# Orders written as tables, weights in four pieces and other gates for the loads in a gated linear attention and MLP kernel

## The chip, the cores and the metric

The kernel runs on one core of one Trainium2 chip. The metric is the time of one execution on the device in microseconds; of several runs the median is given. Profiles show one execution, in microseconds from the start of its span.

## What is computed

Four batches of eight heads, 768 tokens, head size 48. A state of 48 x 48 per head decays by alpha and takes in an outer product at every token; the output of all heads, 3072 tokens of 384 numbers, goes through two layers with a squared relu between them.

```python
for t in range(S):
    state = alpha[:, :, t, :, None] * state + np.einsum('bhd,bhe->bhde', k[:, :, t], v[:, :, t])
    y[:, :, t] = np.einsum('bhd,bhde->bhe', q[:, :, t], state)
...
x = np.ascontiguousarray(attn_out.transpose(0, 2, 1, 3)).reshape(B * S, H * D)
h = x @ w_in            # 384 x 2048
r = np.maximum(h, 0.0)
out = (r * r) @ w_out   # 2048 x 384
```

All inputs and the output are float32 in device memory; the matmuls run in bf16.

## The kernel before

**Units.** The work is cut into 12 units of 256 tokens: three stretches of the sequence, four batches each, in the order stretch 0 of all batches, stretch 1, stretch 2. Names of operations end in the unit's number.

**One unit.** Four loads (`lda`, `ldk`, `ldq`, `ldv`: alpha, k, q, v, 384 KB each). The front takes the logarithm of alpha on ScalarE (`ln`; for most units on the product `pr` of two neighbouring tokens), sums it along the tokens by matmuls (`m1`, `m1i`, `m1s`), takes exponentials (`ei`, `ea`, `ec`, `es`), and multiplies them into k and q on VectorE (`ekm`, `eqm`, with `bk` and `aq` for the neighbouring token). The products are transposed: on TensorE with a copy out of PSUM for units 0 to 2 (`tr`, `et`), by DMA for the others (`tr0_3`, `tr1_3` and so on). `vc` casts v to bf16. Then come the scores (`p`, masked by `mk` on VectorE), the state (`kv`, `sa`, `sc`, `sd`), the output of the attention (`y`, copied out by `xe`) and its transposition (`xt`, `xv`; by DMA from unit 4 on). Unit 0 does its front in two halves of four heads: `ln0_0`, `ln1_0`, `ei0_0` and so on up to the score parts `p0_0` and `p1_0`.

**The two layers of a unit.** The first is eight blocks `s1_g_u` of six matmuls each, into one of two PSUM banks in turn. Each block is emptied by a relu (`re`, ScalarE or VectorE) and squared in pairs or alone (`sq`, VectorE, ScalarE or POOL). The second is eight blocks `s2_g_j_sg` of four matmuls, four for each half j of the tokens, summed in a single PSUM bank `psO` which `oe` empties; then `out` stores it. The last 128 tokens of unit 11 go by two cuts of the columns (line 1012).

**Who decides the order.** Every operation is entered with `add`, with its engine or engines to choose from, a cost and a due time (`prio`). `schedule` plays the program through with these costs, a picture of the DMA rings among them, and picks for each free engine the ready operation with the lowest due time; a table `SHIFT` moves single due times, `BIAS` holds POOL back, and `AFFINITY` lets TensorE go on with one kind of matmul. What comes out is a fixed list for each engine, emitted in that order: on the chip each engine goes through its list and waits at each entry for what it needs. `fill` then puts filler matmuls on zeros (line 1143) into the gaps of TensorE's list, from the landing of the memset of ZERO up to the planned start of the first s1 block. All operations without a name (memsets, masks) are entered first.

**Loads.** The loads of a unit go through SP's queue, except those of unit 2, which POOL issues. The weights are cast from float32 to bf16 in the DMA and so are issued by POOL as well, in `WS` pieces each: `win0`, `win1`, `wout0`, `wout1`. A load or a weight piece can have a gate: another load whose landing it waits for before it is issued (`AFTER`). Every piece of `win` covers `FT / WS` of the 16 blocks of 128 hidden numbers, so s1 blocks 0 to 3 need `win0` and 4 to 7 `win1`; the s2 blocks with sg 0 and 1 need `wout0`, those with 2 and 3 `wout1`.

```python
AFTER = {(1, "v"): (0, "q"), ("win", 0): (1, "a"), ("win", 1): (1, "a"), 2: (1, 'v'), ("wout", 0): (1, 'v'),
         ("wout", 1): (1, 'v'), 3: ("wout", 0)}
AFTER.update({g: (g - 1, "q") for g in range(4, G)})
```

From unit 5 on, a load also waits for the last reader of the unit before (`BEHIND`).

**The list of the start before the change.** TensorE: nine fillers, `m10_0 m11_0`, four fillers, `tr00_0`, fillers, `tr10_0`, fillers, `tr01_0 p0_0 kv0 tr11_0`, fillers, `p1_0 m11`, fillers, `y0`, fillers, `tr0_1 xt0`, fillers, `tr1_1`, fillers, `p0_1 s1_0_0 s1_0_1 kv1 s1_0_2 s1_0_3 y1 s1_0_4 s1_0_5 xt1 s1_0_6 s1_0_7 m1i2 s1_1_0 ...`. POOL: masks, `vc0 win0 win1 sd0 lda2 ldk2 ldq2 ldv2 wout0 wout1 sd1 pr3 sd2 vc4 pr5 vc5 pr6 vc7 vc10`. SP: the eight loads of units 0 and 1, then `lda3 ldk3 ldq3 ldv3 lda4 ldk4 ldq4 ldv4 out0_1 tr0_3 tr1_3 lda5 ...`.

Of the kernel before, what the change touches and what calls it, by code (L numbers as in the profile page):

```python
# [33 lines left out]
class Program:  # L34
# [12 lines left out]
    AFFINITY = 2500

    SHIFT = {
        "aq2": -248, "aq3": -1491, "bk2": 5224, "bk3": -2010, "bk5": 1601, "bk6": -3855, "ea0_0": 13157,  # L50
        "ea1": -1949, "ea1_0": 12558, "ea2": 2000, "ea3": -1980, "ea4": -1414, "ea5": -2487, "ea6": 81,
        "ec0_0": 20747, "ec1": -746, "ec1_0": 11544, "ec2": 2000, "ec3": -2160, "ec4": -1533, "ec5": 2471,
        "ei0_0": 10906, "ei1": -1289, "ei1_0": 11939, "ei2": 2000, "ei3": 8259, "ei4": -2378, "ei5": 98, "ei6": -386,
        "ekm0_0": 11970, "ekm1": -1066, "ekm1_0": 10619, "ekm2": 5424, "ekm3": -1183, "ekm4": 175, "ekm5": 937,
        "ekm6": 1068, "eqm0_0": 12087, "eqm0_3": -1862, "eqm0_4": 3228, "eqm0_5": 3013, "eqm0_6": -440, "eqm1": 2398,
        "eqm1_0": 12786, "eqm1_3": 1310, "eqm1_4": 270, "eqm1_5": -275, "eqm1_6": -211, "eqm2": 2240, "es2": 2000,
        "es3": -2890, "es5": -2113, "es6": -1558, "et00_0": -6783, "et01_0": 2965, "et0_1": 18, "et0_2": 4740,
        "et10_0": 1180, "et11_0": 849, "et1_1": -8121, "et1_2": 9290, "kv0": 1952, "kv1": -5798, "kv2": -10315,
        "lb4": -1797, "lb5": 195, "lb6": 67, "lm4": -1578, "lm5": -1529, "lm6": -1532, "ln0_0": 10550, "ln1": -409,
        "ln1_0": 17073, "ln2": 2000, "ln3": -2160, "ln4": 564, "ln5": 4370, "ln6": -283, "m10_0": 4838, "m11": -338,  # L60
        "m11_0": 9538, "m1i2": 2121, "m1i3": -533, "m1i5": 400, "m1i6": -1147, "m1s2": 2468, "m1s3": 3167,
        "mk0_0": -1001, "mk0_1": 9322, "mk0_2": 5670, "mk0_3": -10630, "mk0_4": 4794, "mk0_5": -4832, "mk1_0": -830,
        "mk1_1": 1380, "mk1_2": 4510, "mk1_3": -10630, "mk1_4": 7108, "mk1_5": -124, "oe0_0": -3484, "oe0_1": -14385,
        "oe1_0": -724, "oe1_1": 2594, "oe2_0": -260, "oe2_1": -627, "oe3_0": 11805, "oe3_1": 30, "oe4_0": -7260,
        "oe4_1": -7260, "oe5_0": 5260, "oe5_1": 5260, "out0_1": -8010, "out1_1": 6560, "out2_1": 2593, "out3_1": 30,
        "out4_1": -7260, "out5_1": 5260, "p0_0": -830, "p0_1": -2249, "p0_2": 4532, "p0_3": -11271, "p0_4": 2163,
        "p0_5": -6910, "p1_0": -830, "pr2": 376, "pr3": 563, "pr4": -2031, "pr5": 4470, "pr6": -3765, "pr7": -5581,
        "re0_0": -253, "re0_1": -2327, "re0_2": -1810, "re0_3": -2805, "re0_4": 7066, "re0_5": -3141, "re0_6": 1463,
        "re0_7": -2710, "re1_0": -2540, "re1_1": -1766, "re1_2": -2620, "re1_3": -2792, "re1_4": 4740, "re1_5": 99,
        "re1_6": -833, "re1_7": 2948, "re2_0": -151, "re2_1": -240, "re2_2": 24, "re2_3": -68, "re2_4": -519,  # L70
        "re2_5": -240, "re2_6": 5363, "re2_7": 3246, "re3_0": -3327, "re3_1": -1860, "re3_2": -1860, "re3_3": -2293,
        "re3_4": -1860, "re3_5": -5935, "re3_6": -6334, "re3_7": -1379, "re4_0": -5850, "re4_1": -2100,
        "re4_2": -6410, "re4_3": -2118, "re4_4": -5850, "re4_5": -5850, "re4_6": -5850, "re4_7": -5850,
        "re5_0": 2020, "re5_1": 2020, "re5_2": 2020, "re5_3": 2020, "re5_4": 2020, "re5_5": 2020, "re5_6": 2020,
        "re5_7": 2020, "s1_0_0": -2767, "s1_0_1": -1766, "s1_0_2": -1810, "s1_0_3": -1898, "s1_0_4": 202,
        "s1_0_5": -2691, "s1_0_6": -5306, "s1_0_7": 405, "s1_1_0": -2620, "s1_1_1": -5074, "s1_1_2": -364,
        "s1_1_3": 596, "s1_1_5": -6169, "s1_1_6": -383, "s1_1_7": -1034, "s1_2_0": -739, "s1_2_1": -687,
        "s1_2_2": -5198, "s1_2_3": -900, "s1_2_4": -1700, "s1_2_5": -240, "s1_2_6": -45, "s1_2_7": -688,
        "s1_3_0": -1860, "s1_3_1": -2146, "s1_3_2": -1582, "s1_3_3": -1860, "s1_3_4": -3211, "s1_3_5": -435,
        "s1_3_6": -1113, "s1_3_7": -1860, "s1_4_0": -10307, "s1_4_1": -5990, "s1_4_2": -5519, "s1_4_3": -6913,  # L80
# [316 lines left out]
def bass_gla_recurrent__then__act_relu_squared_kernel(  # L397
# [777 lines left out]
```

## Time and profile before

| what | value |
|---|---|
| median of 3 runs | 174.92 us (174.46 to 176.85) |
| the profiled execution: own time / span | 176.21 us / 174.5 us |
| busy: TensorE, its weight loads | 169.1 us, 130.5 us |
| busy: VectorE, ScalarE, POOL | 121.3 us, 117.6 us, 18.8 us |
| HBM read, written | 25.17 MB, 4.72 MB |
| queue 1 (loads, stores, transposes), share of 16 DMA engines | 71.4% in 73184 packets |
| queue 0 (issued by POOL's software, the weights among them) | 12.1% in 1536 packets |

Busy time counts a matmul from its start to its end, and matmuls overlap, so the distance from one start to the next says more than the length. A transfer has an issue (an instruction on SP or POOL) and a landing; the view of a tile gives the time between the two. A wait is put down to what ended it last.

### The profile page before, as it was taken

Reading aid. Unit: us, or ns where it says so; the run is one execution under the profiler, and the core shown is the slowest. Engines: PE = TensorE matmul, PEld = TensorE weight load, DVE = VectorE, ACT = ScalarE, POOL = GpSimd, SP = SyncE. Lnnn points to the kernel's source line nnn. Section 1 sums busy time; section 2 is a strip of 40 time slices with the busy share of each in tenths; the row PEclk is TensorE's granted clock in tenths of the full one; section 3 lists DMA queues with packets and bytes.
Section 4 is the critical chain, followed back from the end, with each engine's and each line's share of the span. In section 5 each row is a group of like instructions: output and inputs, shape, how many; then the busy total and the mean of one; then the engine's idle time right before and its main releaser. Section 6 shows DMA issues by size and latency. Waiting matters only on the chain.

```text
span 174.5 us, 5094 instructions
## 1 busy us (share of the span) xinstructions
PE 169.1 (97%) x2237; PEld 130.5 (75%) x2237; DVE 121.3 (70%) x197; ACT 117.6 (67%) x211; POOL 18.8 (11%) x28
## 2 busy tenths in 40 slices
PE   7989999999999999999999999999999999999994
PEld 2556898856886697777788886778788697688773
DVE  5497799797967869866778966868849726322230
ACT  3848698868869569768768757378668564566440
POOL 3159010022102120000100000000200000000000
DMA  5999999979998999798998897999899690040022
GB/s 139 324 297 190 274 303 216 230 208 280 274 229 125 274 235 188 200 222 151 278 212 211 228 196 180 275 201 251 201 214 208 115 196 4 0 135 4 10 80 90
DMA packets 74743, 33.36 MB, mean 191 GB/s; under 512 B 71649, under 2 KB 71905, under 8 KB 74721
## 3 DMA queue, kind: packets, MB, share of 16 engines
q1 hardware_dynamic: 73184, 28.32, 71.4%
q0 software_dynamic: 1536, 4.72, 12.1%
q8 instruction: 17, 0.28, 0.7%
q14 instruction: 6, 0.04, 0.1%
HBM read 25.17 MB, written 4.72 MB: 171 GB/s over the span
## 4 chain that ended last, share of the span: by engine, by line
PE 56%; DMA 26%; ACT 6%; DVE 4%; SPq 3%; POOL 2%; issue 1%
PE psO L1089 22%; PE psWH L1042 22%; DMA raw<-in_v_dram 9%; DMA wout<-in_moe_w_out_dram 8%; DMA raw<-in_alpha_dram 5%; DMA raw<-in_q_dram 5%; SPq L568 3%; PE psO L1143 2%; POOL raw L568 2%; ACT rr L1050 2%; PE psX L843 2%; PE psX L1012 2%; ACT vbf L742 1%; PE psZ L811 1%; PE psX L832 1%; PE psX L940 1%
## 5 line engine op out<-in xcount | busy, mean ns | idle before, releaser
L1042 PE MATMUL psWH<-xt,win 128*128 128x256 bf16 x576 | 73.9, 275 | 0.5 <-ACT rr L1050 0.2
L1042 PEld LDWEIGHTS psWH<-xt,win 128*128 128x128 bf16 x576 | 65.0, 145 | 6.2 <-DVE rr L1052 1.6
L1089 PE MATMUL psO<-wout,gt 128*128 128x384 bf16 x368 | 68.9, 326 | 0.0
L1050 ACT ACTIVATE rr<-psWH 128x512 bf16<-128x512 f32 x83 | 48.9, 596 | 21.5 <-PE psWH L1042 20.0
L1089 PEld LDWEIGHTS psO<-wout,gt 128*128 128x128 bf16 x368 | 34.8, 98 | 18.3 <-DVE gt L1060 0.2
L1060 DVE TENSOR_TENSOR gt<-rr 128x1024 bf16<-128x1024 bf16 (+1 forms) x47 | 28.4, 608 | 25.1 <-ACT rr L1050 24.5
L951 DVE TENSOR_TENSOR pm<-psX,caus 128x1024 bf16<-128x1024 f32 x12 | 14.6, 1220 | 2.4 <-PE psZ L940 2.1
L951 DVE TENSOR_TENSOR pm<-psZ,caus 128x1024 bf16<-128x1024 f32 x12 | 14.6, 1216 | 1.5 <-PE psZ L940 1.4
L1097 ACT ACTIVATE osb<-psO 128x384 f32<-128x384 f32 x19 | 9.3, 489 | 6.8 <-PE psO L1089 6.3
L971 ACT ACTIVATE xbf<-psX 128x768 bf16<-128x768 f32 x12 | 9.7, 806 | 5.0 <-PE psX L832 4.1
L746 DVE TENSOR_TENSOR qks<-raw,eq 128x384 bf16<-128x384 f32 x18 | 10.3, 605 | 3.0 <-DMA raw<-in_q_dram 3.0
L1143 PE MATMUL psO<-zero 128*128 128x512 bf16 (+1 forms) x37 | 10.5, 417 | 1.3 <-DVE zero L489 1.3
L741 POOL CAST vbf<-raw 128x768 bf16<-128x768 f32 x4 | 3.7, 930 | 71.5 <-DMA raw<-in_v_dram 71.5
L1064 ACT ACTIVATE gt<-rr 128x512 bf16<-128x512 bf16 (+1 forms) x13 | 10.8, 828 | 0.4
L751 DVE TENSOR_TENSOR qks<-raw,ek 128x768 bf16<-128x768 f32 x11 | 10.7, 969 | 0.4 <-ACT ek L663 0.3
L1052 DVE TENSOR_SCALAR rr<-psWH 128x512 bf16<-128x512 f32 x13 | 8.9, 687 | 2.0 <-PE psWH L1042 1.6
L742 ACT ACTIVATE vbf<-raw 128x768 bf16<-128x768 f32 x7 | 5.9, 845 | 3.5 <-DMA raw<-in_v_dram 3.5
L717 ACT ACTIVATE la<-raw 128x384 f32<-128x384 f32 x8 | 4.2, 523 | 5.3 <-DMA raw<-in_alpha_dram 5.2
L1143 PEld LDWEIGHTS psO<-zero 128*128 128x128 bf16 x37 | 3.5, 108 | 4.6 <-issue 1.9
L906 DVE TENSOR_TENSOR smd<-psZ,sbd 128x384 bf16<-128x384 f32 x8 | 4.4, 554 | 3.4 <-PE psX L832 3.4
L675 DVE TENSOR_TENSOR prd<-raw 128x384 f32<-128x384 f32 x7 | 4.0, 569 | 2.9 <-DMA raw<-in_alpha_dram 2.9
L678 ACT ACTIVATE lab<-prd 128x384 bf16<-128x384 f32 x10 | 5.2, 520 | 1.1 <-POOL prd L677 0.6
(115 smaller groups left out, 165.9 us busy)
## 6 DMA issues: line engine op xcount, KB each, us to landing
raw<-in_alpha_dram SPq DMA_DIRECT2D x11, 384.0 KB, 4.2
raw<-in_k_dram SPq DMA_DIRECT2D x11, 384.0 KB, 5.1
raw<-in_q_dram SPq DMA_DIRECT2D x11, 384.0 KB, 4.2
raw<-in_v_dram SPq DMA_DIRECT2D x11, 384.0 KB, 4.8
out_dram<-osb SPq DMA_DIRECT2D x11, 384.0 KB, 4.3
win<-in_moe_w_in_dram POOLq DMA_DIRECT2D x2, 768.0 KB, 9.9
wout<-in_moe_w_out_dram POOLq DMA_DIRECT2D x2, 768.0 KB, 15.2
raw<-in_alpha_dram POOLq DMA_DIRECT2D x1, 384.0 KB, 9.7
```

What stands on the lines that cost most here:

```text
L746: add("dve", lambda e, j=j, dst=dst: e.tensor_tensor(dst, RAW[r][:, 2, :, j, :].rearrange("p (n x) d -> p n x d", x=2), EQ[la][:, j].rearr ...
L751: add("dve", lambda e, a=a, E=E: e.tensor_tensor(QKS[qs][:, a, :, :, 0:D], RAW[r][:, 1 + a].rearrange("p h j d -> p j h d"), E[la][:].rear ...
L951: add("dve", lambda e, hf=hf, psT=psT: e.tensor_tensor(PM[pm][:, hf].rearrange("p r n j t -> p (r n) (j t)"), psT[:, :, :].rearrange("p r ...
L971: add("act", lambda e: e.activation(XBF[x2][:], psX[:, :, 0:HD], AF.Copy), act_ns(2 * HD), p0 + 6100, reads=[("ps", "X", 0), ("ps", "X", 1 ...
L1042: ins = pe.matmul(psH[hb][:, i * T:(i + 1) * T], WIN[:, kk, hidden(fj)], mov, start=(kk == 0), stop=(kk == KT - 1))
L1050: add("act", lambda e, hb=hb, rr=rr: e.activation(rr, psH[hb], AF.Relu), act_ns(512), pu + 600, reads=[("ps", "H", hb)], writes=[("rr", rb ...
L1052: alts={"dve": (lambda e, hb=hb, rr=rr: e.tensor_scalar(rr, psH[hb], 0.0, None, ALU.max), dve_ns(512))})
L1060: add("dve", lambda e, dst=dst, sq=sq: e.tensor_tensor(dst, sq, sq, ALU.mult), 148 + k * 267, pu + 1200, reads=[("rr", rb, h) for h in ran ...
L1064: "act": (lambda e, dst=dst, sq=sq: e.activation(dst, sq, AF.Square), act_ns(k * 512))})
L1089: ins = pe.matmul(psS, GT[gt][:, fj, j, :], WOUT[:, fj, :], start=(fj * parts % FT == 0), stop=((fj + 1) * parts % FT == 0))
L1097: add("act", lambda e, j=j, psS=psS: e.activation(OSB[ob][:, j], psS, AF.Copy), act_ns(DM), ps_ + 700, reads=[keyS], writes=[("osb", ob, j ...
L1143: pr.fill(lambda n: lambda pe: pe.matmul(psO[:, 0:n], ZERO[:, 0:128], ZERO[:, 0:n], skip_group_check=True), ((512, 216, 420), (256, 109, 2 ...
```

## The change

The schedule no longer chooses: `ORDERS` names for every engine all its operations in order, and with that which engine does what. `SHIFT`, `BIAS` and `AFFINITY` go. Fillers are put in as before. Operations without a name get `c` and their number (c1 and c3 are the memsets of LAF, c8 to c13 those of the masks, c14 and c15 two of POOL's masks, c19 the memset of ZERO, c20 to c22 POOL's other masks, c23 a copy on ScalarE). Further:

- both weights come in four pieces instead of two (`WS`), with new gates; s1 blocks 0 and 1 now need `win0`, 2 and 3 `win1` and so on, and the s2 blocks with sg 0 to 3 need `wout0` to `wout3`;
- alpha, k and q of unit 0 are loaded in two halves of four heads;
- the gates: `win0` waits for v of unit 0, the other three pieces of `win` for k of unit 1, unit 3 for `wout1` instead of `wout0`, and unit 4 for `wout3` besides q of unit 3;
- the second layer of units 0 and 1 is done in two parts (`IN_HALVES`): first the blocks with sg 0 and 1, copied out by `oe`; after unit 1's first part, those with sg 2 and 3, which `oa` on VectorE adds to what was copied out. Four additions come in.

```diff
+ORDERS = {
+    "pe": """
+        m10_0 m11_0 tr10_0 tr00_0 tr11_0 kv0 p0_0 tr01_0 m11 p1_0 y0 tr0_1 xt0 tr1_1 s1_0_0 s1_0_1 p0_1 s1_0_2 s1_0_3
+        m1i2 kv1 s1_0_4 s1_0_5 y1 s1_0_6 m1s2 s1_0_7 xt1 tr0_2 s1_1_1 s1_1_0 s1_1_3 s1_1_2 tr1_2 s2_0_0_0 s2_0_0_1
+        p0_2 s1_1_5 m1i3 s2_0_1_0 s2_0_1_1 kv2 s1_1_4 m1s3 s2_1_0_0 s2_1_0_1 s1_1_6 s1_1_7 y2 s2_1_1_0 m1i4 xt2
+        s2_1_1_1 s1_2_0 s1_2_1 s2_0_0_2 s1_2_2 s2_0_0_3 s1_2_3 s1_2_4 s2_0_1_2 s2_0_1_3 m1i5 p0_3 s2_1_0_2 s1_2_6
...
+        s1_11_5 s2_10_1_3 s1_11_6 s1_11_7 s2_11_0_0 s2_11_0_1 s2_11_0_2 s2_11_0_3 s2_11_1_0 s2_11_1_1
+    """.split(),
+    "act": """
+        table ln0_0 ei0_0 ea0_0 ln1_0 c23 ei1_0 ea1_0 et10_0 ec1_0 vc0 ec0_0 ln1 et11_0 et01_0 ei1 ea1 ec1 xe0 re0_0
+        re0_1 sq0_1 ln2 re0_2 re0_3 ei2 ea2 ec2 re0_5 xe1 re0_6 es2 re0_7 sq0_7 re1_1 re1_0 et0_2 et1_2 ln3 re1_2 ei3
...
+    "dve": """
+        c8 c16 c11 c12 c7 c13 c5 c10 c1 c9 c3 ekm0_0 c17 c18 c6 eqm0_0 ekm1_0 eqm1_0 et00_0 c19 sa0 sc0 mk0_0 mk1_0
+        ekm1 eqm1 xv0 c2 et1_1 et0_1 pr2 mk1_1 mk0_1 sa1 sc1 re0_4 bk2 ekm2 xv1 c4 sq0_5 eqm2 sq1_1 sd1 re1_3 pr3
...
+    "pool": """
+        c20 c21 c22 c15 c14 win0 lda2 win1 win2 win3 ldk2 wout1 vc1 sd0 ldq2 wout0 sq0_3 ldv2 aq2 wout3 vc2 sq1_3 bk3
+        wout2 pr5 sq2_3 sq1_7 bk5 sd3 sq3_5 sq3_7 vc6 sd5 pr7 sq4_5 sq4_7 sq5_3 bk8 pr9 sq6_1 sq6_3 vc9 pr10 sq7_1
+        vc10 pr11 sq7_7 sd6 sq8_1 bk11 sq8_3 sd7 sq9_3 sq10_7 sq11_3 sq11_5 sq11_7
+    """.split(),
+    "sp": """
+        lda0_0 ldq0_1 lda0_1 ldk0_1 ldk0_0 ldq0_0 ldv0 lda1 ldv1 ldk1 ldq1 lda3 ldq3 ldk3 ldv3 lda4 ldq4 ldk4 lda5
+        tr0_3 tr1_3 ldv4 ldk5 tr0_4 tr1_4 ldq5 ldv5 out1_1 out0_1 lda6 tr0_5 ldk6 tr1_5 ldq6 xt4 ldv6 lda7 ldk7 tr0_6
...
-    BIAS = {"pool": 300}
-    DMA_LAST = {"sp": 800, "act": 800, "pool": 1900}
+    DMA_LAST = {"sp": 800, "act": 800, "pool": 1500}
...
-    AFFINITY = 2500
-
-    SHIFT = {
...
-        op = Op(choices, prio + self.SHIFT.get(name, 0), name)
+        op = Op(choices, prio, name or f"c{len(self.ops)}")
...
+        place = {n: (e, k) for e, names in ORDERS.items() for k, n in enumerate(names)}
+        for op in self.ops:
+            e = place[op.name][0]
+            op.alts = {e: op.alts[e]}
...
-    WS = 2
+    WS = 4
...
-    IN_HALVES = ()
+    IN_HALVES = (0, 1)
     BY_HEADS = (0,)
+    HALF_LOADS = ((0, "a"), (0, "k"), (0, "q"))
...
+            gates = ([load_op[gate] if gate in load_op else named(gate)] if gate else []) + ([load_op["wout", 3]] if g == 4 else []) + ([named(f"{BEHIND[nm]}{g - 1}")] if g >= 5 else [])
+            parts = ((slice(0, 4), (0,), "_0"), (slice(4, 8), (1,), "_1")) if (g, nm) in HALF_LOADS else ((slice(0, 8), (), ""),)
+            for hs, sub, end in parts:
+                load_op[g, nm] = add(ring, lambda e, dst=dst, src=src, hs=hs: e.dma_start(dst[:, hs], src[:, hs]), cost if not sub else 460,
...
-    AFTER = {(1, "v"): (0, "q"), ("win", 0): (1, "a"), ("win", 1): (1, "a"), 2: (1, 'v'), ("wout", 0): (1, 'v'),
-             ("wout", 1): (1, 'v'), 3: ("wout", 0)}
+    AFTER = {(1, 'v'): (0, 'q'), ('win', 0): (0, 'v'), ('win', 1): (1, 'k'), ('win', 2): (1, 'k'), ('win', 3): (1, 'k'), 2: (1, 'v'), ('wout', 0): (1, 'v'), ('wout', 1): (1, 'v'), ('wout', 2): (1, 'v'), ('wout', 3): (1, 'v'), 3: ('wout', 1)}
     AFTER.update({g: (g - 1, "q") for g in range(4, G)})
```

## The prediction

> **What bounds the kernel now.** I read the busy table, the 40 slices, the groups, then the timeline of the first 45 us, the DMA landings and the waits.
>
> ```profile
> PE 169.1 (97%) x2237; PEld 130.5 (75%) x2237; DVE 121.3 (70%) x197; ACT 117.6 (67%) x211; POOL 18.8 (11%) x28
> ...
> DMA  5999999979998999798998897999899690040022
> ...
> L1042 PE MATMUL psWH<-xt,win 128*128 128x256 bf16 x576 | 73.9, 275 | 0.5 <-ACT rr L1050 0.2
> ...
> L1089 PE MATMUL psO<-wout,gt 128*128 128x384 bf16 x368 | 68.9, 326 | 0.0
> ```
>
> TensorE is busy from end to end, but a matmul's 275 ns is its length and not its spacing. The timeline gives the spacing: an s1 block (six L1042 matmuls) starts every 0.655 us, an s2 block (four L1089) every 0.65 us. The dense part starts at 18.46, after fillers have kept TensorE warm:
>
> ```profile
> 16.04 0.56 DVE L998 COPY xt<-psX 128x768 bf16<-128x768 bf16 x1 [0.44 <-PE psX L986]
> 16.61 1.24 PE L1143 MATMUL psO<-zero 128*128 128x512 bf16 x6
> 17.88 0.42 PE L940 MATMUL psX<-kqt 64*64 64x128 bf16 x16
> 18.46 1.53 PE L1042 MATMUL psWH<-xt,win 128*128 128x256 bf16 x12
> ```
>
> xt of unit 0 is ready at 16.60; the first s1 then waits for win0 (landed 17.91, below) and for the scores of unit 1, which stand ahead of it. From 18.46 on I compared each block's distance to the next with the usual one of its kind: s1 96 x 0.655 = 62.9, s2 92 x 0.65 = 59.8, attention, transposes and the cut last tile 23.8, together 146.5. The last block starts at 171.18, so 6.2 us are lost: 2.33 before 44 us, 2.2 between 44 and 110, 1.7 after. Only 11 losses exceed 0.12 us: 1.46 us before 44, 1.45 us after. The rest is about 0.1 at every entry into the small attention matmuls, as many before as after the change. **So the most the new orders can win is 2.9 us, plus what the dense part starts earlier.** Before 44 us the fight is over VectorE and the transfers (VectorE 22.94 of 25.6 us, DMA share 1.00):
>
> ```profile
> 18.40:44.00 25.60, 25.14 (x353) 19.82 (x342) 22.94 (x34) 20.24 (x35) 3.30 (x3) 1.00 1.00 255
> 44.00:136.00 92.00, 91.40 (x1277) 72.32 (x1275) 72.44 (x113) 67.01 (x124) 5.74 (x6) 1.00 1.00 217
> ```
>
> (columns: window, length, busy PE, PEld, DVE, ACT, POOL, clock, DMA share, GB/s.) The weights' landings follow from the tile views: two win halves issued at 9.4 and 10.3, the two wout halves at 16.7 and 17.3.
>
> ```profile
> L539 POOL DMA_DIRECT2D win<-in_moe_w_in_dram x2: 786/862/937, 9.4 to 10.3; - x2
> DMA to landing us min/median/max: 8.5/9.9/11.3
> ```
>
> ```profile
> L539 POOL DMA_DIRECT2D wout<-in_moe_w_out_dram x2: 576/578/581, 16.7 to 17.3; - x2
> DMA to landing us min/median/max: 13.7/15.2/16.8
> ```
>
> So win lands at 17.9 and 21.6, wout at 30.4 and 34.05. By the landings in the trace, the eight loads of units 0 and 1 come 1.2 us apart (4.24 to 12.66), unit 2's at 22.85 to 26.85, unit 4's alpha at 41.84.
>
> **The start, part by part.** *Halves of the loads:* half a load is 0.6 us, so the first logarithm runs at 3.7 instead of 4.33. But k's first half now comes fifth (6.05) and q's sixth (6.65), so the first product starts near 6.1 (6.56 before). *The zero memset* goes from first on VectorE to behind et00_0, some 10 us in, and the fillers need it. What they buy is seen here:
>
> ```profile
> 1.25 4.02 PE L1143 MATMUL psO<-zero 128*128 128x512 bf16 x9 [1.25 <-DVE zero L489]
> 5.07 0.37 PE L590 MATMUL psX<-laf,linc 128*128 128x192 bf16 x1
> 5.23 0.37 PE L591 MATMUL psX<-laf,linc 128*128 128x192 bf16 x1
> ```
>
> The first nine fillers are 0.43 apart and later ones 0.215; the 192-column matmuls go from 0.16 apart to 0.09 within the next microsecond. TensorE thus runs at half rate for its first 4.6 us (1.25 to 5.9), which the clock column (1.00 throughout) doesn't show. With fillers from 10.2 on, full rate comes near 14.8, and m11_0 (+0.35), kv0 (+0.35) and m1 of unit 1 (+0.5) are slow: up to 1 us on the path. *The cast of v0* goes from POOL, where it made a product take 1.21 instead of 0.56, to ScalarE (0.85, rows of L742), in front of kv0. Chain: ei1_0 7.9, ea1_0 8.9, et10_0 9.5, ec1_0, cast to 10.55, kv0 to 11.4 (before: 10.41), then VectorE in its new order sa0, sc0 (0.55 each), mask 1.22, mask 1.21 to 15.0, y0 15.1 (before 13.48), copy, transposes, xv0 to 18.0. At full rate the same chain ends at 17.3. So **s1 starts at 17.3 to 18.05** and not with win0, which lands by 16.45 (issued behind v0 at 7.95, plus at most the 8.5 of a piece twice its size). p0_1 (0.57) now stands behind two s1 blocks, inside the dense part. Net -0.6 to +0.15; I take -0.2.
>
> **The weights.** Each win piece has half the columns, so twice as many packets of half the size. Queue 1 spent 71.4% of 16 engines' span on 73184 packets, 27 ns each; 768 more cost between nothing and 768 x 27 / 16 = 1.3 us. POOL issues win0, lda2, win1-3, ldk2, wout1, ldq2, wout0 in one queue; at 2.0 us a piece, 1.2 a load and 1.5 us from last data to landing: win1 19.5, win2 21.7, win3 24.0, wout1 27.4, wout0 30.4. TensorE's list wants them, from 18.05, at 19.9, 22.0, 24.1 and (wout0) 29.9: waits of 0 to 0.6 each. Four issues more on POOL cost about 0.6 to 0.9 each, covered while it waits for ldk1.
>
> **The gates.** Unit 3's alpha now waits for wout1 (27.4; before, wout0, 30.41). While wout1 still arrived, alpha of unit 3 took 4.84 from issue to landing (30.42 to 35.26), that of unit 4, alone, 3.6 (38.23 to 41.84): SP's queue gives way to POOL's. So it lands between 31.0 and 32.3, product and logarithm add 1.1, and m1i3, wanted at 33.0, waits 0 to 0.4. The Trainium skill (DMA: Bandwidth & Descriptors, Queues, rings and completion order) says that each DMA engine takes turns between queues packet by packet; POOL's packets are larger (4.72 MB in 1536 against 28.32 MB in 73184), so by that rule SP's loads would hardly move before POOL's queue is empty near 33, m1i3 would wait some 2 us and the sum would be +0.8 us instead of -0.7. The trace agrees only in part: 1.2 us were lost, not all of the overlap. Unit 4's waits for wout3. On POOL, wout3 stands behind sq0_3, ldv2 and aq2; aq2 needs es2 (about 26.4), so wout3 is issued at 27.5 and lands at 33.6 if POOL's queue goes first, 36.4 if it shares the engines evenly with unit 3's loads. Alpha of unit 4 lands 3.6 later, 37.2 to 40.0; 1.1 more, and m1i4 is wanted at 40.3. Behind lda4 in SP's queue stand lda5 and both transposes of unit 3. wout2 is behind sq1_3 and bk3, issued near 36.6, landing by 42.5; s2_0_0_2 wants it at 43.8. I take 1.2 us of waits before 44 in place of 1.46: -0.3. The halved second layer adds four additions of 0.56 on VectorE; sq0_3 (1.36 there) and three relus (0.69) leave it, so nothing for these, while s1 and score blocks cover the release of psO.
>
> **The tables later.** POOL takes 20 squares. No row has one: the cast of 768 elements (0.82) gives 1.1 us for 1024, the product of 384 (1.00) gives 2.7; I take 1.9, since the square reads one tensor but computes. A VectorE operation on SBUF that meets POOL doubles (0.56 to 1.21, 0.68 to 1.36): up to 20 x 0.65 = 13 us more on VectorE, whose 72.4 of 92 us leave room for it. Sixteen relus (0.69) arrive for about as many squares. Gain at most 1.45 us, loss bounded by queueing at perhaps 3; -0.4. At the end sq11_7 sits on POOL with s2_11_0_0 to 0_2 (1.95) as cover, where relu 0.6 plus 1.04 follow sq11_5: +0.2.
>
> **Sum:** -0.2 - 0.3 - 0.4 + 0.2 = -0.7. Span 174.5 to 173.8, the profiled execution's own 176.21 to 175.5. The runs shown have a median 1.3 below that execution, so I put 174.92 - 0.7 = **174.2 us**.
>
> **Rivals.**
> *Slower: wout3 and the gate of unit 4.* For: wout3 sits behind computing on POOL, and lda4 can't be issued before it lands; DMA share is 1.00 there. If SP's queue goes first, wout3 lands at 37.5 instead of 36.4, and if a 2.7 us square and an es2 that waits its turn on ScalarE hold its issue 3 us more, at about 40.7: alpha lands at 44.3, m1i4 runs at 45.4, and TensorE stands 5.1 us, of which 0.7 was counted: 174.2 + 4.4 = 178.6. It decides once wout3 lands after 35.6; from there each microsecond costs one. Against: by 36 SP's queue has only the end of unit 3 left. 0.18.
> *Faster: everything fits.* Both wait sums go (2.9) and the chain runs at full rate with s1 from 17.3 (0.6): 174.92 - 3.5 = 171.4, or a little under. Against: eleven waits with different causes would all have to go. 0.10.
> *TensorE stays slow into the dense part*, since fillers are cut by waits: half rate for 4.6 us from 18.05 costs 2.3: 176.5. For: nine early fillers are gone. Against: fillers from 10.2 on fill the same gaps as before. 0.07. The Trainium skill (TensorE: Matmul & The Clock Gate, Part 1: The HAM clock gate) has the array start at half rate, be released after about 3.4 us of sustained work and fall back in an idle stretch of that length. The trace shows the first step, at 4.6 us, and no fall back.
> *Packet by packet*, SP's loads stand still until POOL's queue is empty: m1i3 waits 2 us where I count 0.4, so 174.2 + 1.5 = 175.7, 0.10; half of the overlap lost in the one case seen speaks against it.
>
> **How the numbers follow.** Forecast 0.55 (172.5 to 175.6 alone). Two per cent, about what a measurement of this kernel can tell from no change, is 171.4 to 178.4. Faster 0.10, slower 0.18, within 0.72, with the third and fourth rival. The range goes from 171.3, the faster case, to 177.8, most of the way to the slower one.
>
> **What would show it.** Right: the first L1143 filler near 10, first L1042 at 17.3 to 18.1, cast of unit 0 under ACT, SP waiting on wout before lda4, POOL busy near 50 us, PE losses before 44 near 1.5. Wrong: m1i4 after 43, or L1042 spaced 0.22 at the start, or PE waiting for gt from POOL again and again after 60 us.

## The result, and the profile after: 1.1% slower

The changed kernel takes 177.64 us (median of 22 runs, 175.44 to 181.64), the kernel before, in turn with it on the same chip, 175.05 (174.46 to 178.19). The ratio is 1.0111 with a 95% interval of 1.0088 to 1.0135: slower by 1.1%, where 0.4% faster was forecast. Ratios leave out executions in which TensorE's granted clock fell or the time was far above the kernel's fastest; medians keep them. The profiled execution took 177.45 us with a span of 175.7 (before: 176.21 and 174.5). These two differ by 1.2 us where the ratio stands for 1.9: the profiled execution of the kernel before was itself 1.2 us above its median. What follows accounts for the 1.2.

The page of the changed kernel, busy time, the DMA row of the slices, and the new squares:

```profile
PE 163.9 (93%) x2206; PEld 127.5 (73%) x2206; DVE 120.0 (68%) x186; ACT 107.5 (61%) x197; POOL 63.2 (36%) x61
...
DMA  5999999989998999999979998969988492040004
...
L1059 POOL TENSOR_TENSOR gt<-rr 128x1024 bf16<-128x1024 bf16 (+1 forms) x20 | 32.8, 1643 | 65.2 <-ACT rr L1046 55.9
```

POOL has 33 instructions more, 20 of them squares. VectorE and ScalarE have less to do than before, and still the end comes later. The windows show where TensorE stands against before (25.14 and 91.40 us busy there):

```profile
18.40:44.00 25.60, 25.14 (x383) 19.83 (x381) 21.80 (x35) 19.88 (x37) 11.25 (x11) 1.00 1.05 248
44.00:136.00 92.00, 90.67 (x1273) 71.11 (x1271) 72.03 (x104) 60.30 (x115) 35.01 (x28) 1.00 1.04 214
```

From 18.4 to 44 TensorE is busy for the same time, and the transfer engines have no room in either kernel (DMA share 1.05, before 1.00); POOL has 8 us more to do (11.25 for 3.30), VectorE 1 us less. Counted by distances from block to block as in the prediction, the account of the two profiled executions is:

| | before | after | difference |
|---|---|---|---|
| first s1 block starts | 18.46 | 19.24 | +0.78 |
| work behind it, at usual distances (p0_1, 0.57, among it only after) | 146.48 | 147.18 | +0.70 |
| losses behind it, before 44 us | 2.33 | 2.27 | -0.06 |
| losses behind it, after 44 us | 3.91 | 3.72 | -0.19 |

The sum, +1.23 us, is the difference of the spans (1.2). **In these two executions the whole loss is in the start**: the first block comes 0.78 later, and the scores `p0_1` (0.57), done ahead of it before, are not even done. TensorE's own list of the changed kernel there:

```profile
11.53 0.64 PE L936 MATMUL psX<-kqt 64*64 64x128 bf16 x16
12.51 0.53 PE L646 MATMUL psWH<-laf,linc 128*128 128x384 bf16 x1
...
13.79 0.40 PE L652 MATMUL psWH<-ones,laf 128*128 128x2 bf16 x8
14.12 0.64 PE L936 MATMUL psZ<-kqt 64*64 64x128 bf16 x16
14.70 1.68 PE L1138 MATMUL psO<-zero 128*128 128x512 bf16 x4
16.30 0.36 PE L868 MATMUL psX<-smd,kqt 128*64 128x96 bf16 x8
```

The first filler (L1138) comes at 14.70, and its four matmuls stand 0.4 apart: TensorE is still at half rate, and everything ahead of it was (a score group takes 0.64, in the kernel before 0.42). The trace's own records of the granted clock begin with a rise to full rate at 16.24; ahead of its first record the clock column prints 1.00 all the same, and the trace of the kernel before holds no record at all. The sums of unit 1 (L646 to L652, `m11`) take 1.6 us instead of 1.0, and the second half of the scores (14.12) stands behind them. So its mask ends at 16.04 and y0 runs at 16.30, 2.8 us later than before. VectorE tells of a second limit (after, then the same product before):

```profile
15.95 1.08 DVE L747 TENSOR_TENSOR qks<-raw,ek 128x768 bf16<-128x768 f32 x1
17.16 1.37 DVE L747 TENSOR_TENSOR qks<-raw,eq 128x768 bf16<-128x768 f32 x1
17.69 1.52 POOL L911 TENSOR_TENSOR sbd<-tmp,acm 128x384 bf16<-128x384 f32 x1
18.62 0.56 DVE L994 COPY xt<-psX 128x768 bf16<-128x768 bf16 x1
```

```profile
14.64 0.95 DVE L751 TENSOR_TENSOR qks<-raw,eq 128x768 bf16<-128x768 f32 x1
```

The copy that releases s1 (`xv0`, L994) could start at 18.59, when xt0 is done. Ahead of it in VectorE's list stands `eqm1`, the product with q of unit 1, which ended at 18.53. That q landed at 17.07 (before: 11.53). It was issued at 8.93 instead of 6.64, since v of unit 1 now stands ahead of k and q and the half loads of unit 0 come about 1 us late, and from 9.15 POOL's win0, later lda2, shared the transfers with it: 8.1 us from issue to landing instead of 4.9.

```profile
L564 SPq DMA_DIRECT2D raw<-in_q_dram x1: 1151/1151/1151, 8.9 to 8.9; - x1
DMA to landing us min/median/max: 8.1/8.1/8.1
```

VectorE was busy with `ekm1` to 17.03, though, so in this execution the landing held `eqm1` for 0.1 us only; it would have held it for longer behind earlier masks. Beside POOL's `sd0` (L911) the product then took 1.37 us instead of 0.95. Two limits of different kinds thus end within 0.1 us of each other.

### The profile page after: what moved, and what is told of

The parts are those of the page before. It is cut to its first block, busy times and chain, and to the rows that moved or that the text cites. A ratio compares the mean times of both kernels' runs of the same rounds, so it can differ in the third digit from the quotient of the medians.

```text
span 175.7 us, 5071 instructions
## 1 busy us (share of the span) xinstructions
PE 163.9 (93%) x2206; PEld 127.5 (73%) x2206; DVE 120.0 (68%) x186; ACT 107.5 (61%) x197; POOL 63.2 (36%) x61
## 4 chain that ended last, share of the span: by engine, by line
PE 78%; DMA 11%; DVE 5%; ACT 2%; SPq 1%; issue 1%; DVEq 0%
PE psWH L1038 32%; PE psO L1085 29%; DMA raw<-in_k_dram 6%; DMA kqt<-qks 3%; DMA raw<-in_q_dram 2%; PE psX L936 2%; PE psZ L807 2%; PE psX L839 2%; PE psX L1008 2%; DVE qks L747 1%; PE psZ L936 1%; PE psX L828 1%; DVE pm L947 1%; PE psWH L680 1%; SPq L564 1%; PE psO L1138 1%
## 5 line engine op out<-in xcount | busy, mean ns | idle before, releaser
L1038 PEld LDWEIGHTS psWH<-xt,win 128*128 128x128 bf16 x576 | 61.7, 114 | 7.0 <-DVE xt L994 1.0
L1059 POOL TENSOR_TENSOR gt<-rr 128x1024 bf16<-128x1024 bf16 (+1 forms) x20 | 32.8, 1643 | 65.2 <-ACT rr L1046 55.9
L1046 ACT ACTIVATE rr<-psWH 128x512 bf16<-128x512 f32 x67 | 39.0, 593 | 23.9 <-PE psWH L1038 23.4
L1048 DVE TENSOR_SCALAR rr<-psWH 128x512 bf16<-128x512 f32 x29 | 19.8, 688 | 14.9 <-PE psWH L1038 14.5
L1060 ACT ACTIVATE gt<-rr 128x1024 bf16<-128x1024 bf16 (+1 forms) x22 | 18.9, 859 | 1.3 <-DVE rr L1048 1.1
L1056 DVE TENSOR_TENSOR gt<-rr 128x1024 bf16<-128x1024 bf16 (+1 forms) x18 | 12.1, 672 | 4.8 <-ACT rr L1046 4.8
L673 POOL TENSOR_TENSOR prd<-raw 128x384 f32<-128x384 f32 x5 | 5.0, 1000 | 19.4 <-DMA raw<-in_alpha_dram 19.4
L1095 DVE COPY osb<-psO 128x384 f32<-128x384 f32 x6 | 3.3, 556 | 4.5 <-PE psO L1085 3.5
L936 PE MATMUL psX<-kqt 64*64 64x128 bf16 x192 | 5.2, 229 | 1.0 <-DVE tmp L909 1.0
L717 ACT ACTIVATE eq<-la 128x384 f32<-128x384 f32 x8 | 4.2, 520 | 3.2 <-DVE la L715 3.0
```

The source lines that it names most:

```text
L936: ins = pe.matmul(psT[64 * c:64 * c + 64, rr_, o:o + 128], keys, mov)
L1038: ins = pe.matmul(psH[hb][:, i * T:(i + 1) * T], WIN[:, kk, hidden(fj)], mov, start=(kk == 0), stop=(kk == KT - 1))
L1046: add("act", lambda e, hb=hb, rr=rr: e.activation(rr, psH[hb], AF.Relu), act_ns(512), pu + 600, reads=[("ps", "H", hb)], writes=[("rr", rb ...
L1048: alts={"dve": (lambda e, hb=hb, rr=rr: e.tensor_scalar(rr, psH[hb], 0.0, None, ALU.max), dve_ns(512))})
L1056: add("dve", lambda e, dst=dst, sq=sq: e.tensor_tensor(dst, sq, sq, ALU.mult), 148 + k * 267, pu + 1200, reads=[("rr", rb, h) for h in ran ...
L1059: alts={"pool": (lambda e, dst=dst, sq=sq: e.tensor_tensor(dst, sq, sq, ALU.mult), 200 + k * 840), "act": (lambda e, dst=dst, sq=sq: e.act ...
```

## Experiments

Every ratio is to the kernel before, run in turn with it. Operations are named as in the tables.

**Theory 1:** the late start costs it, since TensorE is cold. **Rivals:** the half loads and the landing of q of unit 1; squares on POOL that stretch VectorE's instructions; later, **theory 2:** the transfers, full from 8 to 44 us, take back whatever the start wins.

### The changed kernel again

> The changed kernel again, beside the others on the same chip. Every theory expects what was measured of it: a ratio of 1.009 to 1.014 to the kernel before, s1_0_0 at 19.2 us, and p0_5 late by 1.1 us at 71 us. If the loads of unit 1 land by chance in another order in this run (k at 16.4 instead of 12.5 us), s1_0_0 stands at 20 us or later.

Ratio 1.0139 (1.0032 to 1.0246). The profiled execution, 181.02 us, was the longest of four (the shortest took 177.84); it shows one way in which a long execution comes about, and does not explain the 1.1%. TensorE reached the full rate at 13.30 already, y0 ran at 15.46, and still the first block came at 20.97, since q of unit 1 landed at 19.03:

```profile
20.14 1.04 PE L770 MATMUL psZ<-ident,qks 128*128 128x128 bf16 x8 [2.28 <-DVE qks L747]
20.97 2.74 PE L1038 MATMUL psWH<-xt,win 128*128 128x256 bf16 x12
```

TensorE stood 2.28 us for `eqm1`, which had waited 2.59 us for q, and then 12 matmuls took 2.74 us instead of 1.50. The windows (columns as before, the clock after POOL) say why:

```profile
20.00:21.00 1.00, 0.86 (x9) 0.86 (x10) 0.62 (x3) 0.00 (x0) 0.00 (x0) 0.56 1.22 194
21.00:22.00 1.00, 1.00 (x7) 0.72 (x6) 0.79 (x2) 0.00 (x0) 0.00 (x0) 0.50 1.24 206
```

The granted clock fell to 0.50 for 3.4 us (20.13 to 23.54). In this execution the late load costs twice: the wait, and a slow TensorE behind it.

### The cold start by itself

```diff
 # kernel before, its own lists as tables
-        c19 c8 c9 ... ekm0_0 eqm0_0 et00_0 ekm1_0
+        c8 c9 ... ekm0_0 eqm0_0 et00_0 c19 ekm1_0      # c19: memset of ZERO, VectorE
```

> The kernel before with its own order written out as tables, every instruction where it was, and only the memset of the zero operand moved from first place on VectorE to the place behind et00_0 (where the changed kernel has it; fill matmuls ahead of it fall away). Theory 1 (a TensorE that did nothing before the first matmuls runs at half rate to 14 or 15 us, and that is the larger part of the late start): y0 moves from 13.48 to 14.3 or later, the prefixes and scores ahead of it take twice as long, and the start of the dense part moves by 0.3 to 1.0 us (18.8 to 19.5), ratio 1.002 to 1.007. Rival (the half rate is hidden behind the first weight piece, which lands at 17.9): s1_0_0 stays at 18.4 to 18.5 and the ratio at 1.000.

s1_0_0 at 19.56 instead of 18.46, y0 at 14.66 instead of 13.48, what lies behind it 0.2 us longer (152.95 us from the first block's start to the last one's, before 152.72), span 175.8 instead of 174.5. The clock's rise is recorded at 13.09. TensorE's list of this kernel:

```profile
8.46 1.03 PE L1150 MATMUL psO<-zero 128*128 128x512 bf16 x2 [0.27 <-DVE zero L496]
9.85 0.64 PE L947 MATMUL psX<-kqt 64*64 64x128 bf16 x16
10.42 0.82 PE L818 MATMUL psWH<-vbf,qks 64*128 64x96 bf16 x16
```

The state update (L818) takes 0.82 us here and in the changed kernel, and took 0.51 before. The measured ratio is 1.0038 (0.9997 to 1.0079): 0.7 us where the change lost 1.9, at the edge of what can be told from nothing, though the profile shows the delay itself at 1.1. win0, landed at 17.3, hid nothing of it: p0_1 ran at 18.99, behind six fillers. An earlier try let the planner make new lists with the late memset and so moved more than the memset:

> The kernel before with one change: the memset of ZERO comes behind et00_0, near 8 us, so that the nine first fillers go. Theory COLD (half rate at the start is lost time in itself): y0 moves from 13.5 to 14.5 or later, the first s1 block from 18.46 to 19.2 or later, the span grows by 0.7 us or more. Theory CAUGHT (the start is held by weights and by the loads, cold work hides behind them): y0 moves by the same, but win0 lands at 17.9 and the scores of unit 1 come at 17.9 to 18.3 as before, so that the span grows by less than 0.4 us.

Ratio 1.0276 (1.0201 to 1.035), s1_0_0 at 19.38, but also new waits, at 28, 73 (1.5 us) and 98 us. It says nothing on the memset alone.

### Undoing parts of the start in the changed kernel

```diff
 # a_zero_first: VectorE
-        c8 c16 ... et00_0 c19 sa0
+        c19 c8 c16 ... et00_0 sa0
 # a_whole_loads: SP
-        lda0_0 ldq0_1 lda0_1 ldk0_1 ldk0_0 ldq0_0 ldv0 lda1
+        lda0 ldk0 ldq0 ldv0 lda1
 # a_start_all: both, and vc0 from ScalarE to POOL, ahead of win0
```

> The changed kernel with one move: the memset of ZERO is first on VectorE again, so that fillers run from about 1.3 us. Theory COLD (the new order leaves TensorE at half rate until 16 us, and that holds the start back): m1 of unit 1 takes 0.8 us instead of 1.61, the first s1 block starts at 17.6 to 18.2 instead of 19.24, the span falls by 0.7 to 1.2 us (less than the start gains, since the pieces of win at 19.8, 21.7 and 23.6 come next), and runs lie closer together. Theory LOADS (half loads land late) or CAST (cast of v0 on ScalarE): the start moves by less than 0.4 us.

Ratio 1.0248 (1.0129 to 1.0367): nothing won, and by these few runs (178.92 to 182.58) rather more lost. In the profiled execution, the longest of the four, y0 ran at 15.06, 1.24 earlier, but k of unit 1 landed at 16.38 (12.48 in the changed kernel's profile) and q at 19.37; TensorE stood 2.4 us for `eqm1`, and s1_0_0 came at 21.82.

> The changed kernel with unit 0 loaded in whole tensors in the order alpha, k, q, v. Theory LOADS: v of unit 0 lands at 7.9 instead of 8.85, k at 5.4 instead of 7.07, the first s1 block starts 0.6 to 1.0 us earlier, the span falls by 0.4 to 0.9. Theory COLD: the loads are not what the chain waits for after 9 us, the start moves by less than 0.4 us and TensorE is still at half rate until about 16 us.

Ratio 1.0199 (1.0118 to 1.0281). q landed at 16.17, 0.9 earlier, and s1_0_0 stayed at 19.29. The masks, late as before, ended at 15.92, and `ekm1` and `eqm1` behind them took 1.43 and 1.58 us beside POOL's `vc1` and `sd0` (0.95 each in the kernel before), so VectorE reached xv0 at 18.68: with one limit eased, others held. Waits of 1.2 us for a transposition by DMA at 98 us and 0.5 at 50 are new and not explained.

> The changed kernel with the whole start undone: ZERO first, whole loads of unit 0, cast of v0 on POOL ahead of win0. If the loss sits in the start (COLD, LOADS and CAST together), the first s1 block starts at 16.3 to 17.3, the span falls by 1.2 to 1.8 us and the kernel is level with the one before or up to 0.4 per cent faster. Rival DENSE (the loss sits in the tables behind the start, POOL's squares among them): the start gains, the end does not, span within 0.5 us of the changed kernel.

Ratio 1.0065 (1.0026 to 1.0103), the only one of the three below the change, though the intervals overlap: q at 14.48, s1_0_0 at 18.61, 0.63 earlier. But y0 ran at 15.56, still 2.1 us later than before, with TensorE at full rate since 7.20: the cold start is not all of y0's delay, and the new order of the lists is left as the likely rest. And m1i3 now waited 1.77 us, since alpha of unit 3 landed at 34.51 instead of 32.73.

### q of unit 1 freed from POOL's transfers

```diff
 # a_gate_k1
-    ('win', 0): (0, 'v')
+    ('win', 0): (1, 'k')
 # a_start_before: a_start_all, and
-        lda1 ldv1 ldk1 ldq1          ('win', 0): (0, 'v')
+        lda1 ldk1 ldq1 ldv1          ('win', 0): (1, 'a')
 # a_start_sc5: a_start_before, and xv0 ahead of eqm1, sc5 ahead of ekm6 (VectorE)
```

> The changed kernel with one gate moved: win0 waits for k of unit 1 instead of v of unit 0. Theory CAUGHT (the weights that POOL issues at 9 us overtake SP's loads of k and q of unit 1; how far varies from run to run, and win1 to win3 wait for that k): k of unit 1 lands near 12.5 in every run and never at 16, as it did in the run with ZERO first; win0 is issued near 12.6 and lands near 19, so that the first s1 block comes at 19.5 to 20.5, but runs lie within 2 us of each other (the changed kernel: 175.4 to 181.6) and the median is at or under that of the changed kernel. Rival (the spread has another cause, such as the clock): the spread stays at 4 us or more and the median rises by the later start, about 1 us.

q landed at 13.69, win0 at 18.25, and all that POOL issues landed 1 to 3.4 us later: s1_0_0 at 19.95, alpha of unit 3 at 37.16, m1i3 waited 2.6. Ratio 1.0254 (1.0138 to 1.0369).

> The changed kernel with ZERO first, cast of v0 on POOL, whole loads of unit 0 and, beyond the run that undid these, the order alpha, k, q, v for unit 1 too and win0 waiting for alpha of unit 1, as before the change. Theory CAUGHT: all eight loads land by 12.8 (k of unit 1 at 10.3, q at 11.5), the first s1 block comes at 16.8 to 17.6, runs lie close together; then the first layer catches up with win1 to win3 (near 20, 22, 24) and unit 3's first sum waits 1 to 2 us for its alpha, which is behind POOL's weights; end level with the kernel before, ratio 0.995 to 1.005. Theory COLD or CAST: no gain over the run that undid the start (ratio 1.0065).

q at 11.54, s1_0_0 at 18.20; alpha of unit 3 at 35.29, m1i3 waited 2.2. Ratio 1.0217 (1.0113 to 1.0321).

> As the run with the start of before, and on VectorE xv0 ahead of eqm1 and sc5 ahead of ekm6. If the wait of p0_5 (1.15 us at 71 us) and xv0's wait behind eqm1 are lost time of their own, the span is 0.8 to 1.6 us shorter than in that run and the kernel is 0.3 to 1.0 per cent faster than before. If what is won is given back to the next transfer, it is within 0.4 us of that run.

Ratio 1.0127 (1.0044 to 1.0209). xv0 ran at 17.15, but s1_0_0 stands behind `tr1_1`, which needs `eqm1`, now the later of the two: 19.55. VectorE's order there can't be mended from one side.

### The whole start of the kernel before

```diff
 # h_start: the five lists up to tr1_1, xe0, xv0, win0, ldv1 as before the change;
 #          HALF_LOADS = (); ('win', 0): (1, 'a'); all behind it as changed
 # h_start_fix: h_start, and
-         3: ('wout', 1)}                           ekm6 lb6 sc5
+         3: ('wout', 1), (3, 'a'): ('win', 3)}     sc5 ekm6 lb6
```

> The changed kernel with the start of the kernel before on all five queues, up to the first transposed activations (whole loads in the old order, memset of zero first, cast of v on GpSimd, first weight piece behind alpha of unit 1), and everything behind it as changed (four weight pieces, halves, gate of unit 4, tables). Theory 1 (the start costs 0.8 us and the rest of the change is even): y0 at 13.5 to 14, s1_0_0 at 17.5 to 18.3, ratio 1.000 to 1.006, that is 1.3 us or more less than the changed kernel. Rival (transfers set the dense part, so an earlier start only waits at 33 us for alpha of unit 3): s1_0_0 just as early, but m1i3 waits 2 us or more for a landing after 34 us, the same time as the changed kernel within 0.5 us, ratio 1.009 to 1.014.

s1_0_0 at 16.30: 2.9 us earlier than in the changed kernel. And the time: ratio 1.019 (1.0103 to 1.0278), span 178.2. Losses behind the first layer's start nearly doubled: from the first block's start to the last one's it took 158.57 us, in the changed kernel 153.17, and nearly 5 of these 5.4 us come before 44. The waits of TensorE from 18 to 44 us (line, what it waited for, sum, times, longest):

```profile
PE psZ L782 <- DVE qks L759: 1.8, 1, 1.8
PE psWH L1050 <- DMA win<-in_moe_w_in_dram: 1.7, 2, 1.5
PE psWH L692 <- ACT lab L686: 1.4, 1, 1.4
```

Three transfers: k of unit 2 (landed 26.45), win1 (19.67), alpha of unit 3 (35.11). Here are 8 to 44 us of the kernel before, of the changed kernel and of h_start, the last two numbers being DMA share and GB/s:

```profile
8.00:44.00 36.00, 34.95 (x528) 25.91 (x525) 30.93 (x45) 26.96 (x47) 11.23 (x13) 1.00 1.04 252
```

```profile
8.00:44.00 36.00, 34.12 (x514) 25.69 (x515) 29.77 (x46) 26.31 (x50) 18.76 (x19) 1.00 1.07 252
```

```profile
8.00:44.00 36.00, 30.73 (x500) 23.14 (x499) 27.46 (x40) 23.21 (x42) 18.44 (x20) 1.00 1.08 247
```

The transfers are full in all three and move the same. h_start's were even started later: POOL's first load of unit 2 is released by v of unit 1, second in the changed kernel's order (11.31) and fourth here (13.03), and what stands behind it in POOL's queue, down to `wout0`, is issued 0.4 to 1.7 us later than in the changed kernel; k of unit 2 and `wout1` landed 1.8 and 1.7 us later, the others within 0.7.

> h_start with two waits taken away: alpha of unit 3 is released by the fourth piece of the first weights (23.6 us) instead of the first piece of the second (26.4), and the scaling sc5 stands ahead of the product ekm6 on VectorE. Theory 1 with its two dense causes: alpha of unit 3 lands by 31.5, m1i3 waits under 0.5, p0_5 waits under 0.2, ratio 0.992 to 0.999, below the kernel before. Rival (each removed wait is taken up by the next transfer or VectorE instruction in the row): the ratio is within 0.003 of h_start's.

Ratio 1.0205 (1.0117 to 1.0292), nothing gained. alpha of unit 3, issued 4.3 us earlier (23.89), landed at 34.95, as in h_start, 2.6 us behind POOL's last load of unit 2 (32.37), which was issued after it. The wait at p0_5 went, and a new one of 1.06 us stood at 100.

> h_start with the loads of unit 2 (and with them all that GpSimd issues behind) released by q of unit 1 (lands 11.8) instead of v of unit 1 (13.0). Theory 2: GpSimd's transfers start 1.2 us earlier and all land that much earlier, but v of unit 1 comes later (16 to 19 us); the waits at s1_0_2, tr0_2 and m1i3 (1.5, 2.0 and 1.6 us) fall by up to 1.2 each, and the span by 1 to 2.5 us, 175.5 to 177. Rival: bytes are only moved, v of unit 1 or alpha of unit 3 lands later, and the span stays at 178.

Ratio 1.0262 (1.0174 to 1.0351). POOL started 1.4 us earlier (11.89), and k of unit 2 landed at 25.19; alpha of unit 3 gained 0.5 us only (34.58), and m1i3 waited 2.59. win0 came 1.1 us later (17.23), and s1_0_0 with it (17.36). The rival held.

### Fewer bytes

```diff
 # h_less and h_less_again: h_start, and for wout0 and wout1
+            rest = dst[:, cutn:]
+            dst, src = dst[:, :cutn], src[:, :cutn]
+            add("pool", lambda e: e.memset(rest, 0.0), ...)
```

> h_start, but the first two pieces of the second weights are read only by half (the other half of their buffer is set to zero by GpSimd at the start; 1.5 KB less for each partition and piece, so this kernel leaves a part of the weights out). Theory 2 (from 8 to 44 us the 16 transfer engines are always busy, and what is won at the start is waited for at the loads of unit 2 and 3): everything behind the two pieces lands up to 3 us earlier, alpha of unit 3 at 32 to 33 us instead of 35.1, m1i3 waits under 0.3 us instead of 1.6, and the span falls from 178.2 to 175.5 to 177. Rival (the orders on the engines set the pace): alpha of unit 3 lands earlier, but m1i3 stays at 36 and the span within 0.5 us.

> h_less once more, for its profile (half of two pieces of the second weights left out, 0.8 MB in all). Theory 2: alpha of unit 3 lands at 32 to 33 us (35.1 in h_start), m1i3 waits under 0.5 us, losses behind the first layer 8 to 10 us instead of 11.8, span 175 to 177. Rival (orders on the engines): alpha of unit 3 earlier, losses within 0.7 us of h_start's, and the shorter time of h_less came from elsewhere.

Ratios 1.0054 (0.9996 to 1.0113) and 1.0097 (1.0053 to 1.0142), against h_start's 1.019 (1.0103 to 1.0278): the intervals touch, but 16 of these 20 executions took less than the shortest of h_start (179.70). Taking away 0.8 MB of reads thus brought back about 1 to 1.4%, some 2 us, with nothing else done to the engines but two memsets on POOL. alpha of unit 3 landed at 31.09, 4.0 us earlier, and the wait for it was gone from the list. That is what theory 2 asks for. The profiled execution of h_less_again lost the gain again in a 3.1 us wait for win1, and took 180.42 us where the shortest of its runs took 176.44; the effect rests on the times, and no profile shows where a shorter execution wins it.

### Another order of the same bytes

```diff
 # h_order: h_gate, and
 # POOL
-        ... win3 ldk2 wout1 vc1 sd0 ldq2 wout0 ...
+        ... win3 ldk2 ldq2 lda3 wout1 vc1 sd0 wout0 ...
 # TensorE: s1_1_5 m1i3 ahead of s2_0_0_0
 # h_order_sq: vc1 ahead of lda3; the 20 squares of POOL on VectorE
```

> h_gate with alpha of unit 3 on GpSimd's queue, behind q of unit 2 and ahead of both pieces of the second weights, q of unit 2 ahead of them too, and s1_1_5 and m1i3 ahead of s2_0_0_0 on TensorE. Theory 2: alpha of unit 3 lands at 27 to 29 us, m1i3 does not wait, the two weight pieces land at 29 to 32 and s2_0_0_0 waits up to 1.5 us for them; span 173 to 175.5, ratio 0.985 to 1.0, the shortest of all. Rival (the bytes ahead of 44 us are the same, so another transfer is waited for, v of unit 2 or the weight pieces): the sum of the waits is as in h_gate, ratio 1.005 to 1.015.

> h_order with the cast of v of unit 1 ahead of the waiting load of alpha of unit 3 on GpSimd, and the 20 squares of GpSimd on VectorE as in a_sq_dve. If the order of the bytes is what matters: no wait of kv1, alpha of unit 3 at 28 us, no wait of m1i3, losses behind the first layer 6 to 8 us instead of 14.5, span 172 to 174.5, ratio 0.985 to 1.0. If only the sum of the bytes matters: s2_0_0_0 waits 1.5 us or more for the second weights and kv2 for v of unit 2, losses 9 to 11 us, ratio 1.003 to 1.015.

Ratios 1.0377 (1.0309 to 1.0445) and 1.0303 (1.0212 to 1.0394): both much slower. alpha of unit 3 came at 27.8 and 27.7, as meant. In h_order the cast `vc1` stood behind its waiting issue:

```profile
PE psZ L819 <- POOL vbf L749: 5.0, 1, 5.0
```

With that mended, TensorE waited 2.3 us for ScalarE ahead of m1s2 (`acm`, L707), 1.5 for win1, and some 4 us more in smaller pieces. No version that was run beats the kernel before.

### The wait at 71 us and POOL's squares

The largest single wait of the changed kernel is p0_5, for `sc5` (L909). VectorE's list there, and POOL's:

```profile
68.59 2.38 DVE L747 TENSOR_TENSOR qks<-raw,ek 128x768 bf16<-128x768 f32 x1 [1.07 <-DMA raw<-in_k_dram]
71.37 0.54 DVE L909 TENSOR_TENSOR tmp<-psZ,smd 128x384 f32<-128x384 f32 x1
```

```profile
68.27 1.90 POOL L1059 TENSOR_TENSOR gt<-rr 128x1024 bf16<-128x1024 bf16 x1 [15.29 <-ACT rr L1046]
```

`ekm6` waits for k of unit 6, then takes 2.38 us beside a square on POOL, and `sc5` stands behind it and `lb6`.

```diff
 # a_sc5: VectorE
-        ... bk6 sq3_3 ekm6 lb6 sc5 eqm1_6
+        ... bk6 sq3_3 sc5 ekm6 lb6 eqm1_6
 # a_sq_dve: the 20 squares of POOL in VectorE's list, at their planned times
```

> The changed kernel with one move on VectorE: sc5 stands ahead of ekm6 instead of behind lb6. In the changed kernel p0_5 on TensorE waits 1.15 us at 71 us for sc5, which stands behind ekm6, which waits for k of unit 6 (landed 68.50) and then takes 2.38 us beside a square on POOL. Theory BLOCK (that one wait is lost time): the span falls by 0.8 to 1.2 us, the start stays at 19.2. Rival GIVEN BACK (the next limit follows at once, the transposes of unit 5 landing at 69.5 and the loads behind): the span falls by less than 0.4 us.

The profiled execution had no wait at p0_5, losses 5.53 and span 175.0; its other runs took 180.1 to 182.3, too far apart for a ratio. Inconclusive.

> The changed kernel with its 20 squares on GpSimd (32.8 us) put on VectorE instead, each at the planned place. Theory 1 (a square on GpSimd stretches the VectorE instruction beside it, ekm6 2.38 instead of 0.95 us, and that makes p0_5 wait 1.15): ekm6 0.95 to 1.1, no wait at p0_5, losses behind the first layer down by 0.5 to 1.5 us, ratio 1.002 to 1.008. Rival (VectorE, 120 us busy, gets 10 to 15 us more and is late elsewhere): losses up by 1 us or more, ratio above 1.015.

Ratio 1.0076 (1.0021 to 1.013). The same product in this kernel:

```profile
66.69 0.95 DVE L752 TENSOR_TENSOR qks<-raw,ek 128x768 bf16<-128x768 f32 x1
```

0.95 us, no wait at p0_5, losses 4.97, span 174.5, with 6.8 us more on VectorE and 31 us less on POOL. Part of that need not be the squares: k of unit 6 landed 2.6 us earlier than in the changed kernel (65.88), where the work beside it stood 0.7 earlier (m1i6 at 64.65 and 65.31). The interval overlaps that of the changed kernel, so what the squares on POOL cost in time, if anything, is not shown.

## Why the prediction was wrong

**The step that failed is the start**: "Net -0.6 to +0.15; I take -0.2", measured +0.78 and +0.57 for p0_1, together +1.35. Its first term, half a load in 0.6 us, held but for one gap of 1.6 us between two of the halves; so k's first half landed at 7.07 (forecast 6.05), the first product ran at 7.16 (6.1), and v of unit 0, and with it the issue of win0, came at 8.85 and 9.15 (7.95). The slack ahead of the cast took most of this up, and to the state update the working held (cast until 10.55 forecast, 10.73 measured; kv0 until 11.4 and 11.60). Then it broke at three places. It let the two masks follow each other and end at 15.0. In truth the second scores stand behind `m11` on TensorE, which started at 12.51 and ran at half rate, so the second mask ended at 16.04. It had the fillers begin at 10.2 and the full rate near 14.8; the first filler ran at 14.70, since the list held none ahead of it, and the rate rose at 16.24. And it followed one chain: that q of unit 1 is issued 2.3 us later and then shares the transfers with POOL's first pieces, and that `ekm1` and `eqm1` stand ahead of `xv0` and are stretched by POOL's `vc1` and `sd0`, was not looked at; the prediction has a price for such a meeting (0.56 to 1.21), but did not set it for these. The bound on s1 (17.3 to 18.05) was made for one of two limits. The cold TensorE alone is worth 1.1 us of the first block's start in the kernel before (b_cold); how the rest splits between q, POOL and the new order can't be told, since easing one leaves the others. Nor did a better start win the time back: h_start began its first block 2.9 us earlier than the changed kernel and had a ratio of 1.019. The account says where the time went in two executions; that the start alone is the cause is not shown.

**Waits before 44** (-0.3): -0.06. The weights' landings were right, mostly within 0.5 us: win1, 2 and 3 forecast at 19.5, 21.7, 24.0 and seen at 19.80, 21.66, 23.57; wout1 27.4 and 26.41; wout0 30.4 and 30.52; wout3 33.6 to 36.4 and 35.67; wout1 and wout2 (42.5 and 43.59) missed by 1. Two terms of that sum were wrong all the same: in the kernel before the last packet of a weight's half ended 0.3 us ahead of its landing, not 1.5 (21.36 and 21.63, 33.74 and 34.05), and the packets on POOL's queue grew by 1088, not 768. alpha of unit 3 came 0.4 after its range (32.73), that of unit 4 as much (40.41). **Tables later and the tail** (-0.4 and +0.2): -0.19 together, the sum as forecast, but by luck: -0.13 ahead of 120 us and -0.06 behind it, where +0.2 was expected. The square on POOL is 1.90 us, as chosen, but a meeting with VectorE cost up to 1.4 us and not 0.65; the wait behind it, 1.15 us at 71, is larger than all that the tables won. Work at usual distances grew by 0.13 beyond p0_1, which was not counted.

**Rivals.** The slow one, wout3 and the gate of unit 4, did not happen: wout3 landed at its point of decision (35.67), and m1i4 ran at 42.04, earlier than before. TensorE slow into the dense part did not happen in the execution that stands for the result, but did in after_copy's, behind a wait. Packet by packet was dismissed too easily. In the changed kernel's profile m1i3 hardly waited; but SP's load of q took 8.1 us beside POOL's queue, and in eleven kernels alpha of unit 3 landed 1.0 to 3.7 us after POOL's last load of unit 2. In three others (after_copy, a_zero_first, a_whole_loads), where that load was issued just behind alpha, alpha landed 1.2 to 2.4 us ahead of it; and in eight of the eleven wout3 was still under way on POOL's queue when alpha landed. So SP's loads can lose much beside POOL's, but they do not stand still until POOL's queue is empty; neither rule fits all traces.

**What stays open:** what decides from run to run whether k and q of unit 1 land ahead of POOL's pieces or behind them; the waits of about 1 us near 100 us that come and go in the kernels with a changed start; and whether lists made anew for an earlier start could beat the kernel before. Lists fixed for other landings were tried in eleven versions and did not.

## What to carry to other kernels

Follow every instruction that stands ahead of the first big block, on each engine's list, and price the two or three latest; here the start was set by several of different kinds, and mending one showed little. Before working on an early wait, read the DMA share of the stage behind it: where the transfers were full (h_start), what was won ahead of them was waited for at the next loads. And an order written as a table can turn a load that lands 2 us late into a wait of TensorE and a slower clock (after_copy).

## What the runs showed of the hardware that was not expected

- Six of the profiled executions had the granted clock of TensorE fall to 0.50 on the way, for 3.41 us each (6.83 in a_zero_first). In every trace that holds records the changes lie whole multiples of 3.41 us apart: in after_copy up at 13.30, down at 20.13, up at 23.54. Cut into steps of that length, all six falls come at the end of a step in which TensorE was busy for 0.24 to 1.23 us, and no step at full rate with 1.57 us or more brought one. So a wait of 2.28 us inside one step (after_copy, 1.11 us busy) was enough, and one of 2.40 us in h_gate, which lies across two (1.78 and 2.65 us busy), was not. The Trainium skill (TensorE: Matmul & The Clock Gate, Part 1: The HAM clock gate) has the array fall back after an idle window of about 3.4 us, freely running; the traces agree with the length, but a step need not be idle throughout.
- These steps lie differently in each execution: with the same lists, the changed kernel's clock rose at 16.24 in one profile and at 13.30 in the other.
- One execution of h_less, the profiled one, took 939 us: every s1 matmul was 0.7 to 1.2 us long from the first to the last, and TensorE was busy throughout. Its trace holds no record of the clock, so the 1.00 that the view prints says nothing. None of its other nine runs took more than 179.4. No cause was found.

```profile
L1055 PE MATMUL psWH<-xt,win x576: 707/981/1158, 66.8 to 902.6; 128*128 128x256 bf16 x192
```
